# Loading p in one transfer and half of a k tile in fp32 by another queue, at the start of a packed-attention and token-mixing kernel

## The chip, the cores and the metric

The kernel runs on one core of one Trainium2 chip. The metric is the time of one launch in device microseconds, the median of several runs. A profile is one execution taken by the hardware profiler; its times count from the first instruction of that execution. The engines are TensorE (PE: matrix products; PEld: its weight loads), VectorE (DVE), ScalarE (ACT), GpSimd (POOL) and SyncE (SP). SyncE, ScalarE and GpSimd each issue transfers to a queue of their own; all queues are served by the core's 16 DMA engines.

## The reference

Two stages follow each other for 8 batches, 8 heads, 576 rows, head size 64 and 32 packing queries per head:

```python
p_packed = sm_attn(p, k, v)             # softmax(p k^T / 8) v : 32 rows per head
out      = sm_attn(q, p_packed, p_packed)
x = out.transpose(0, 2, 1, 3).reshape(8, 576, 512)
wq = x @ w_q; wk = x @ w_k              # 512 -> 64
W_tok = einsum('bsd,btd->bst', wq, wk) / 8
mixed = einsum('bst,btd->bsd', W_tok, x)
return maximum(mixed, 0) @ w_out        # float32, (8, 576, 512)
```

Inputs are float32; the kernel computes in bf16 with float32 accumulation.

## The kernel before

Everything is laid out by hand. `ORDER` is one long list of steps; each step is a name, indices, the engine that does it (`@V` VectorE, `@A` ScalarE, `@P` GpSimd, `@S` SyncE) and, after `=`, the PSUM banks. The loop at the end of the function issues the steps in that order, and each engine runs its own in that order; semaphores do the rest. Nothing is scheduled by a planner. Work of neighbouring batches is interleaved in the list, up to three batches deep.

The steps of one batch b, in their own order: `LD.k`, `LD.v`, `LD.q` load (GpSimd's queue casts fp32 to bf16 on the way); `KT` transposes k in blocks of 32 on VectorE; `S1` (line 282) makes the scores of p against k on TensorE; `X1` (line 293) takes the exponential on ScalarE; `TE` transposes it on VectorE; `PV` (line 315) multiplies with v; `RC` and `PP` normalise; `PT` transposes the packed result; `QK` multiplies it with the two small weights; `QV` transposes q; `S2`, `X2`, `RS`, `RR`, `AM`, `AT`, `AE` do the second attention; `WKQ`, `GM`, `Y`, `MX`, `RL`, `OT` (line 540), `OE`, `ST` the token mixing and the store. Stores on SyncE's queue are held until the last v has been loaded (`HOLD.v7`).

The part that the change touches is the start, before the scores of batch 0:

- p, 512 KB in fp32, is loaded once for all batches into a tile `p32` of 128 partitions x 1,024 elements (line 161) in two transfers: `LD.N0` on ScalarE's queue and `LD.N1` on SyncE's, 128 rows of 2 KB each. The source's extents are 16 (4 heads x 4 quarters of the 32 queries), 8 (batches) and 512 elements.
- `NC.0` on VectorE and `NC.1` on ScalarE cast a half each to bf16 (helper, lines 128 and 132); `PX.0` and `PX.1` (line 237) transpose the halves into `pT`, which the scores of all batches use.
- The two small weights follow on the same two queues: `LD.W0` on ScalarE's, `LD.W1` on SyncE's (line 164). GpSimd casts them in `WC.1` and `WC.0`, and stands still until they are there.
- k of batch 0 comes in two halves, both by GpSimd's queue: `LD.h0` (line 168) and `LD.g0` (line 157), then v, the two halves of q, and k of batch 1. `KT.0.0` and `KT.0.1` transpose the halves. `S1.0` needs both halves after its first two products.
- After its weight casts GpSimd issues k of batch 2, v of batch 1 and q of batch 1 (`LD.q1`, line 182), with fillings of constants between.
- `WARM.4=0` and `WARM.22.128=0` (line 619) are products of a constant tile with itself, one of 512 columns and 22 of 128, ahead of `S1.0`; further such fillings stand between the steps of batch 0, the next of them `WARM.8=4` between `S1.0` and `PV.0`.

Of the kernel before, what the change touches and what calls it, by code (L numbers as in the profile page):

```python
# [7 lines left out]
NL, NB, NO, NE = 4, 3, 6, 2  # L8
# [2 lines left out]
OHC = (0, 384), (384, 512)  # L11

ORDER = """
LD.N0@A LD.N1@S SET.warm@V SET.v0@V SET.aT0@V SET.aT1@V SET.aT2@V SET.idf@V LD.W0@A LD.W1@S SET.tab@A LD.h0
LD.g0 LD.v0 LD.r0 LD.q0 LD.k1 NC.0@V PX.0@V NC.1@A PX.1@V SET.aff@P SET.idb@V SET.v3@P KT.0.0@V SET.mask@P
WC.1@P WC.0@P LD.k2 SET.v1@P LD.v1 SET.v2@P KT.0.1@V WARM.4=0 WARM.22.128=0 S1.0=0,1,2,3 X1.0.1@A TE.0.1@V
X1.0.0@A TE.0.0@V WARM.8=4 PV.0.0=4,5 PV.0.1 RC.0@V PP.0.0@V PP.0.1@V LD.q1 PT.0@V WARM.6=6 QK.0=6 QKE.0@A
QV.0.0@V QV.0.1@V QD.0@P WARM.4=7 S2.0.2=2,3 X2.0.2@A RS.0.2@V RR.0.2@V S2.0.0=0,1 LD.v2 S2.0.1=4,5 X2.0.0@A
RS.0.0@V RR.0.0@V X2.0.1@A RS.0.1@V RR.0.1@V AM.0.2@P WARM.6=7 AT.0.2=7 AE.0.2@A AM.0.0@P WARM.5=6 AT.0.0=6
KT.1.2@V AM.0.1@P WARM.3=2 AT.0.1=7 AE.0.1@A AE.0.0@V WKQ.0.0=2,3 WKQ.0.2 WE.0.0@A LD.q2 WKQ.0.1 KT.2.2@V  # L20
S1.1=0,1,4,5 WE.0.1@A GM.0=6 X1.1.0@A TE.1.0@V GE.0@A WARM.2=7 Y.0=2,3 YE.0@V S1.2=0,1,6,7 MR.0=2,3 X1.1.1@A
TE.1.1@V MX.0.0=4,5 X1.2.0@A LD.O PV.1.0=0,1 TE.2.0@V PV.1.1 X1.2.1@A TE.2.1@V RC.1@V LD.k3 PP.1.0@V PP.1.1@V
PT.1@V MX.0.1=6,7 QV.1.2@V RLR.0@A QK.1=2 QKE.1@V RL.0.0@A WARM.3=3 S2.1.2=4,5 S2.1.0=0,1 RL.0.1@A X2.1.2@A
RS.1.2@V RR.1.2@V S2.1.1=2,3 X2.1.0@A RS.1.0@V RR.1.0@V WARM.1=6 PV.2.0=6,7 PV.2.1 X2.1.1@A RS.1.1@V RC.2@V
LD.v3 QD.1@P AM.1.2@P AT.1.2=4 RR.1.1@V AM.1.0@P WARM.5=5 AT.1.0=5 AM.1.1@P LD.k4 PP.2.0@V AE.1.2@A PP.2.1@V
PT.2@V QK.2=4 AE.1.0@A QKE.2@A QD.2@P QV.2.2@V LD.q3 LD.v4 AT.1.1=0 AE.1.1@A WKQ.1.0=2,3 WKQ.1.2 WKQ.1.1
WE.1.0@V S2.2.2=6,7 WE.1.1@A X2.2.2@A S2.2.3=4,5 X2.2.3@A GM.1=1 OT.0.0=2,3 GE.1@V Y.1=6,7 OT.0.1 YE.1@A
RS.2.4@V OE.0.0@A MR.1=0,1 MX.1.1=4,5 RLR.1@A RR.2.4@V OT.0.2=6,7 LD.q4 OT.0.3 KT.3.2@V AM.2.3@P OE.0.1@V
RL.1.1@A S1.3=2,3,0,1 X1.3.0@A AM.2.2@P OT.1.4=4 TE.3.0@V LD.k5 AT.2.2=5 X1.3.1@A TE.3.1@V AT.2.3=2 AE.2.3@V
LD.v5 MX.1.0=6,7 AE.2.2@V PV.3.0=0,1 PV.3.1 OEF.1.4@A WKQ.2.0=2,3 WKQ.2.1 RC.3@V PP.3.1@V RL.1.0@A WKQ.2.2  # L30
WE.2.2@A OT.1.2=4,5 OT.1.3 PP.3.0@V PT.3@V QK.3=6 OE.1.1@A LD.q5 KT.4.2@V S1.4=0,1,2,3 GM.2=7 OT.1.0=4,5
X1.4.1@A LD.k6 GE.2@A QKE.3@V X1.4.0@A QV.3.2@V TE.4.1@V Y.2=2,3 YE.2@A S2.3.2=6,7 X2.3.2@A S2.3.3=0,1
X2.3.3@A MX.2.0=2,3 TE.4.0@V RL.2.0@A MR.2=6,7 RLR.2@V OT.1.1 MX.2.1=6,7 RL.2.1@A OE.1.0@A PV.4.0=0,1 QD.3@P
PV.4.1 RS.3.4@V RR.3.4@V LD.v6 AM.3.3@P AM.3.2@P RC.4@V OT.2.0=2,3 OT.2.1 LD.q6 OE.2.0@A PP.4.0@V PP.4.1@V
PT.4@V QK.4=6 AT.3.3=7 QV.4.2@V AT.3.2=0 AE.3.2@A LD.k7 S2.4.2=4,5 AE.3.3@V X2.4.2@A S2.4.3=2,3 X2.4.3@A
# [25 lines left out]
def kernel(  # L61
# [27 lines left out]
    P = 128  # L89
# [64 lines left out]
    def load(x, eng):  # L154
        a, b = x[0], x[1:]
        if a == "g":
            nc.gpsimd.dma_start(k_in[0][:, 1], pairs(k, 0)[:, 1])
        elif a == "N":
            i, n = int(b), L * Dh // 4
            src = p.rearrange("b (i c) (z l) d -> i (c z) b (l d)", i=2, z=4)  # L160
            (nc.sync if eng == "S" else nc.scalar).dma_start(p32[:, i * n:(i + 1) * n], src[i])
        elif a == "W":
            w = (moe_w_k, moe_w_q)[int(b)].rearrange("(i c j e) m -> (c j) i (e m)", i=2, c=4, e=2)
            (nc.sync if eng == "S" else nc.scalar).dma_start(w32[:, int(b)], w)
        elif a == "O":
            nc.gpsimd.dma_start(wout, moe_w_out.rearrange("(j a) n -> a j n", a=P))
        elif a == "h":
            nc.gpsimd.dma_start(k_in[0][:, 0], pairs(k, 0)[:, 0])
        elif a == "v":
            b = int(b)  # L170
            for i in range(2):
                src = v[b, 4 * i:4 * i + 4].rearrange("c (g r) d -> g c (r d)", r=R)
                nc.gpsimd.dma_start(v_bufs[b % NL][halves(i), 0:7:2], src)  # L173
        elif a == "k":
            b = int(b)
            nc.gpsimd.dma_start(k_in[b % NL], pairs(k, b))
        elif a == "r" or x in ("q0", "q7"):
            b, i = int(b), int(a == "q")
            nc.gpsimd.dma_start(q_in[b % NL][:, i], pairs(q, b)[:, i])
        else:  # L180
            b = int(b)
            nc.gpsimd.dma_start(q_in[b % NL], pairs(q, b))
# [385 lines left out]

    def hold(x):
        b = int(x[1])  # L570
        src = {"k": k_in, "h": k_in, "q": q_in, "r": q_in, "v": v_bufs}[x[0]][b % NL]
        src = src[64:96, 4, 0:2] if x[0] == "v" else src[64:96, 0 if x[0] == "r" else 1, 0:2]
        z = 2 * int(x[0] == "h")
        nc.sync.dma_start(touch[:, z:z + 2], src)
# [78 lines left out]
```

## Time and profile before

| | |
|---|---|
| median of 3 runs | 104.46 us (104.32 to 104.92) |
| span of the profiled execution | 102.8 us |
| busy: TensorE, VectorE, ScalarE, GpSimd | 92.7, 73.7, 65.0, 51.8 us |
| bytes moved by the DMA engines | 25.13 MB, mean 244 GB/s |
| first product of the scores of batch 0 that uses k's second half | 10.18 us |
| batch 1's q landed | 27.48 us |

The profiled execution's own time is not listed apart from its span: the span runs from the first to the last instruction, and the timed runs are longer by what lies around it (104.46 against 102.8 us). In the rows of the profile a start and a length are given in us; `[idle before <-releaser]` is how long the engine stood still before the instruction, and what ended that. GB/s counts what the DMA engines write; a load that casts reads twice as much.

### The profile page before, as it was taken

What the parts mean: (1) busy time and instruction counts of PE and PEld (TensorE: products, weight loads), DVE (VectorE), ACT (ScalarE), POOL (GpSimd) and SP (SyncE); (2) the same over time, 40 slices, a digit from 0 to 9 for tenths busy, and PEclk for the clock granted to TensorE, in tenths of its full rate; (3) what the DMA queues carried; (4) which work ended last, traced back from release to release, by engine and by line L of the source; (5) the groups of instructions that cost most, each with busy time, mean ns of one, the idle gap of its engine ahead of it and who ended that gap; (6) DMA issues with size and microseconds to landing.
All of it is one profiled execution on the core that took longest, in us unless ns stands there. A gap on an engine that the chain in (4) does not pass through costs nothing.

```text
span 102.8 us, 3593 instructions
## 1 busy us (share of the span) xinstructions
PE 92.7 (90%) x1536; PEld 54.6 (53%) x1536; DVE 73.7 (72%) x140; ACT 65.0 (63%) x111; POOL 51.8 (50%) x81
## 2 busy tenths in 40 slices
PE   5995999998698899999998899989999999999940
PEld 3894454555364733655546556643757664743420
DVE  4173366966979479898597979689999979339520
ACT  2320406168853767938986979897889897735540
POOL 5971866993029938925349574558615009100000
PEclk9999999999999999999999999999999999999999
DMA  0999999999999999999999999999999999986894
GB/s 9 249 230 207 213 210 213 207 209 213 205 211 207 212 211 210 213 205 212 211 212 207 211 213 204 217 211 203 255 262 409 411 410 408 418 345 264 335 364 160
DMA packets 13279, 25.13 MB, mean 244 GB/s; under 512 B 1040, under 2 KB 6416, under 8 KB 13008
## 3 DMA queue, kind: packets, MB, share of 16 engines
q0 software_dynamic: 9648, 17.04, 84.0%
q1 hardware_dynamic: 3056, 7.41, 19.0%
q10 hardware_dynamic: 560, 0.46, 1.7%
q8 instruction: 12, 0.20, 0.7%
q14 instruction: 3, 0.02, 0.1%
HBM read 30.15 MB, written 9.44 MB: 385 GB/s over the span
## 4 chain that ended last, share of the span: by engine, by line
PE 49%; DMA 21%; DVE 8%; POOL 7%; ACT 6%; issue 3%; SPq 1%; DVEq 0%; POOLq 0%; ACTq 0%
PE ps L540 26%; DMA q_sb<-in_q_dram 13%; DMA o<-in_moe_w_q_dram 8%; PE ps L373 4%; POOL a L405 4%; PE ps L315 3%; ACT e1T L293 3%; PE ps L419 3%; PE ps L446 3%; DVE rs L394 2%; PE ps L441 2%; PE ps L467 2%; PE ps L282 2%; ACT e L378 1%; DVE qT L237 1%
## 5 line engine op out<-in xcount | busy, mean ns | idle before, releaser
L540 PE MATMUL ps<-wout,relu 128*128 128x512 bf16 x124 | 30.6, 380 | 0.0
L405 POOL TENSOR_TENSOR a<-e,rr 128x256 bf16<-128x256 f32 (+2 forms) x18 | 19.5, 1099 | 17.9 <-DVE rr L399 7.0
L619 PE MATMUL ps<-o 128*128 128x128 f32 (+3 forms) x76 | 19.5, 401 | 1.2 <-DVE o L135 1.2
L540 PEld LDWEIGHTS <-relu 128*128 128x128 bf16 x124 | 10.7, 98 | 11.7 <-issue 1.1
L128 ACT ACTIVATE o<-ps 128x1024 f32<-128x1024 f32 (+2 forms) x13 | 11.3, 871 | 5.4 <-PE ps L540 5.2
L619 PEld LDWEIGHTS ps<-o 128*128 128x128 f32 x76 | 11.3, 209 | 5.2 <-issue 3.6
L503 ACT ACTIVATE relu<-ps 128x1024 bf16<-128x1024 f32 (+1 forms) x14 | 13.0, 968 | 1.1 <-PE ps L492 1.1
L293 ACT ACTIVATE e1T<-ps 128x576 bf16<-128x576 f32 x16 | 9.8, 656 | 5.8 <-PE ps L282 5.2
L378 ACT ACTIVATE e<-ps 128x256 f32<-128x256 f32 (+2 forms) x19 | 11.2, 623 | 2.7 <-PE ps L373 2.5
L394 DVE TENSOR_REDUCE rs<-e 128x16 f32<-128x512 f32 (+2 forms) x13 | 10.9, 840 | 2.3 <-ACT e L378 2.2
L237 DVE STREAM_TRANSPOSE kT<-k_sb 128x1152 uint32<-128x1152 uint32 (+1 forms) x9 | 11.1, 1230 | 1.9 <-DMA k_sb<-in_k_dram 1.9
L173 POOL DMA_DIRECT2D v_sb<-in_v_dram x16 | 10.0, 628 | 4.0 <-DMA v_sb<-in_v_dram 1.6
L237 DVE STREAM_TRANSPOSE qT<-q_sb 128x1152 uint32<-128x1152 uint32 (+1 forms) x10 | 11.0, 1108 | 0.1
L132 DVE COPY o<-ps 128x1024 f32<-128x1024 f32 (+2 forms) x7 | 6.8, 977 | 5.3 <-PE ps L540 2.7
L237 DVE STREAM_TRANSPOSE e<-e1T 128x288 uint32<-128x288 uint32 x16 | 7.4, 468 | 3.1 <-ACT e1T L293 2.7
L128 ACT ACTIVATE aT<-ps 128x128 bf16<-128x128 f32 (+2 forms) x11 | 5.0, 465 | 5.7 <-PE ps L419 3.3
L128 ACT ACTIVATE wkq<-ps 128x448 bf16<-128x448 f32 (+1 forms) x10 | 7.2, 730 | 1.8 <-PE ps L446 1.7
L315 PE MATMUL ps<-v_sb,e 64*64 64x192 bf16 x288 | 7.5, 245 | 0.8 <-DVE e L237 0.5
L315 PEld LDWEIGHTS <-e 64*64 64x64 bf16 x288 | 5.9, 107 | 2.6 <-DVE e L237 2.1
L373 PEld LDWEIGHTS <-qT 64*128 64x128 bf16 x320 | 5.4, 94 | 2.8 <-DVE qT L237 1.7
L373 PE MATMUL ps<-ppT,qT 64*128 64x64 bf16 x320 | 6.6, 190 | 0.2 <-DVE qT L237 0.2
L446 PE MATMUL ps<-aT,pqk 128*128 128x256 bf16 (+1 forms) x48 | 6.8, 246 | 0.0
(70 smaller groups left out, 130.3 us busy)
## 6 DMA issues: line engine op xcount, KB each, us to landing
v_sb<-in_v_dram POOLq DMA_DIRECT2D x16, 288.0 KB, 13.9
out_dram<-o SPq DMA_DIRECT2D x9, 512.0 KB, 9.3
k_sb<-in_k_dram POOLq DMA_DIRECT2D x7, 576.0 KB, 13.6
q_sb<-in_q_dram POOLq DMA_DIRECT2D x6, 576.0 KB, 13.6
out_dram<-o POOLq DMA_DIRECT2D x2, 1024.0 KB, 11.3
out_dram<-o SPq DMA_DIRECT2D x5, 256.0 KB, 2.5
q_sb<-in_q_dram POOLq DMA_DIRECT2D x4, 288.0 KB, 10.4
out_dram<-orem SPq DMA_DIRECT2D x3, 256.0 KB, 8.5
```

The lines of the kernel that those rows point to most:

```text
L128: nc.scalar.activation(o, i, COPY)
L173: nc.gpsimd.dma_start(v_bufs[b % NL][halves(i), 0:7:2], src)
L237: nc.vector.transpose(o, i)
L293: nc.scalar.activation(e1T[:, x], T["s1", b][x].rearrange("a c m -> a m c"), EXP, scale=scale)
L315: nc.tensor.matmul(T["pv", b][halves(cc), i], lhsT, rhs, start=n == 0, stop=n == R - 1, skip_group_check=True)
L373: nc.tensor.matmul(ps[:, y, t - t0, i], lhsT, rhs, start=e == 0, stop=e == 1)
L378: nc.scalar.activation(e2[:, t0:t1].rearrange("a t (i y n) -> a y (t i) n", i=2, y=2), T["s2", b, c].rearrange("a y t i n -> a y (t i) n") ...
L394: nc.vector.tensor_reduce(rs[:, t0 * H:t1 * H], src, axis=AX, op=ADD)
L405: e.tensor_tensor(a2[:, t0:t1].rearrange("a t i (u l) -> a (t i u) l", l=L), e2v(b, c), T["rr", b][:, t0 * H:t1 * H].to_broadcast((P, (t1 ...
L503: nc.scalar.activation(o, i, RELU)
L540: nc.tensor.matmul(ps, lhsT, wout[:, j, :], start=j == 0, stop=j == NJ - 1)
L619: nc.tensor.matmul(bank(int(bk), [w]), warm[:, 0:P], rhs, start=True, stop=True)
```

## The change

p is loaded by one transfer on ScalarE's queue, `LD.N`, with rows of 4 KB. The source's extents are then 8 (4 heads x 2 halves of the 32 queries), 16 (batches x 2 groups of heads) and 1,024 elements. The transposes `PX` read and write in the matching order; `PX.0` and `PX.1` both still handle half of the elements each, and `NC.0`, `NC.1` stay as they were.

The first half of batch 0's k is loaded in fp32 by SyncE's queue (`LD.H0`, 128 rows of 4,608 B) into `h32`, a part of an output tile that is free until batch 4, and cast to bf16 by ScalarE (`HC`, 128 x 1,152), after its cast of p. GpSimd's queue has one issue less and begins with k's second half. SyncE's weight transfer now stands behind half of k instead of half of p, ScalarE's behind all of p.

22 filling products of 128 columns ahead of the scores become 17. The rest of `ORDER` is the same.

```diff
-LD.N0@A LD.N1@S SET.warm@V ... LD.W0@A LD.W1@S SET.tab@A LD.h0
-LD.g0 LD.v0 LD.r0 LD.q0 LD.k1 NC.0@V PX.0@V NC.1@A PX.1@V SET.aff@P SET.idb@V ...
-... WARM.4=0 WARM.22.128=0 S1.0=0,1,2,3 ...
+LD.N@A LD.H0@S SET.warm@V ... LD.W0@A LD.W1@S SET.tab@A LD.g0 LD.v0
+LD.r0 LD.q0 LD.k1 NC.0@V NC.1@A PX.0@V PX.1@V HC@A SET.aff@P SET.idb@V ...
+... WARM.4=0 WARM.17.128=0 S1.0=0,1,2,3 ...
...
-            i, n = int(b), L * Dh // 4
-            src = p.rearrange("b (i c) (z l) d -> i (c z) b (l d)", i=2, z=4)
-            (nc.sync if eng == "S" else nc.scalar).dma_start(p32[:, i * n:(i + 1) * n], src[i])
+            src = p.rearrange("b (i c) (z l) d -> (c z) (b i) (l d)", i=2, z=2)
+            (nc.sync if eng == "S" else nc.scalar).dma_start(p32, src)
+        elif a == "H":
+            (nc.sync if eng == "S" else nc.scalar).dma_start(h32, pairs(k, 0)[:, 0])
...
-        elif a == "h":
-            nc.gpsimd.dma_start(k_in[0][:, 0], pairs(k, 0)[:, 0])
...
+    h32 = spare[:, 0:RQ * Dh]
...
-               .rearrange("a (b i z l) -> a i l z b", b=B, i=2, z=4)[:, x],
-               pbf.bitcast(u32).rearrange("a (i l z b) -> a i l z b", i=2, b=B, z=4)[:, x])
+               .rearrange("a (u z x l) -> a x l z u", u=2 * B, z=2, x=2)[:, x],
+               pbf.bitcast(u32).rearrange("a (x l z u) -> a x l z u", x=2, z=2, u=2 * B)[:, x])
+
+    def HC(eng, bk):
+        copy(eng, k_in[0][:, 0], h32)
```

More of the change, by code (lines that the diff above doesn't have):

```diff
@@ L13 @@
 ORDER = """
[L14 to L23, printed above, removed]
@@ L54 @@
-STF.6.3 YE.7@A ST.5.0 MR.7=6,7 RLR.7@A MX.7.0=4,5 RLF.7.0.1@A RLF.7.0.0@V MX.7.1=2,3 RLF.7.1.0@A OT.7.4=0
-OEF.7.4@A ST.7.4 RLF.7.1.1@V OT.7.1=6 OEF.7.1@V OT.7.0=7 STF.7.1 OT.7.2=1 OEF.7.0@A OH.7.0=0 STF.7.0 OEF.7.2@A
-STF.7.2 OEH.7.0@V STH.7.0 OH.7.1=5 OEH.7.1@A STH.7.1@A
+LD.N@A LD.H0@S SET.warm@V SET.v0@V SET.aT0@V SET.aT1@V SET.aT2@V SET.idf@V LD.W0@A LD.W1@S SET.tab@A LD.g0 LD.v0
+LD.r0 LD.q0 LD.k1 NC.0@V NC.1@A PX.0@V PX.1@V HC@A SET.aff@P SET.idb@V SET.v3@P KT.0.0@V SET.mask@P WC.1@P WC.0@P
@@ L57 @@
+WKQ.7.1 WE.7.0@A WE.7.1@A STF.6.2 OT.6.0=6,7 OT.6.1 GM.7=0 OE.6.0@V OT.5.1 OE.5.0@V ST.5.1 GE.7@A Y.7=4,5 OT.6.3
+OEF.6.3@V ST.6.0 STF.6.3 YE.7@A ST.5.0 MR.7=6,7 RLR.7@A MX.7.0=4,5 RLF.7.0.1@A RLF.7.0.0@V MX.7.1=2,3 RLF.7.1.0@A
+OT.7.4=0 OEF.7.4@A ST.7.4 RLF.7.1.1@V OT.7.1=6 OEF.7.1@V OT.7.0=7 STF.7.1 OT.7.2=1 OEF.7.0@A OH.7.0=0 STF.7.0
+OEF.7.2@A STF.7.2 OEH.7.0@V STH.7.0 OH.7.1=5 OEH.7.1@A STH.7.1@A
 """
@@ L570, in hold @@
         b = int(x[1])
[L571 removed]
+        src = {"k": k_in, "q": q_in, "r": q_in, "v": v_bufs}[x[0]][b % NL]
         src = src[64:96, 4, 0:2] if x[0] == "v" else src[64:96, 0 if x[0] == "r" else 1, 0:2]
[L573 to L574 removed]
+        nc.sync.dma_start(touch[:, 0:2], src)
     def OH(b, h, eng, bk):
```

65 lines of the change are left out of this document (35 added, 30 removed).

## The prediction

> **What bounds the kernel now.** I read the page first, then the chain that ended last, then the start of the timeline, then the DMA by stretches of a microsecond.
>
> ```profile
> span 102.8 us, 3593 instructions
> PE 92.7 (90%) x1536; PEld 54.6 (53%) x1536; DVE 73.7 (72%) x140; ACT 65.0 (63%) x111; POOL 51.8 (50%) x81
> GB/s 9 249 230 207 213 210 213 207 209 213 205 211 207 212 211 210 213 205 212 211 212 207 211 213 204 217 211 203 255 262 409 411 410 408 418 345 264 335 364 160
> q10 hardware_dynamic: 560, 0.46, 1.7%
> 13.89 13.59 DMA q_sb<-in_q_dram
> 27.48 0.02 issue
> 27.51 1.39 DVE qT L237
> ...
> 98.09 0.67 PE ps L580 x4
> ```
>
> The first four lines are the page's; the rest is the chain (start, length, what). TensorE (PE) is busy 90% of the span, and after 28.9 us nearly every piece of the chain is compute: no load ends a step there. Before it there is one long piece, the load of batch 1's q, which lands at 27.48. The loads run at about 210 GB/s from the second slice on. That counts what is written, and a casting load writes half of what it reads. Stores reach 410 GB/s. So both cases move about 410 GB/s, and a load that sits in a full queue comes when the bytes ahead of it are through, not when it was issued.
>
> Is that load the only thing that ends there? The timeline of VectorE (DVE) just before, and the chain's start on all engines:
>
> ```profile
> 27.14 0.31 DVE L237 STREAM_TRANSPOSE ppT<-pp 128x128 uint32<-128x128 uint32 x1
> 0.73 0.65 ACTq L161 DMA_DIRECT2D o<-in_p_dram  x1
> 0.74 0.68 SPq L161 DMA_DIRECT2D o<-in_p_dram  x1
> 1.27 0.73 POOL L168 DMA_DIRECT2D k_sb<-in_k_dram  x1 [0.82 <-POOLq L637]
> 3.06 5.60 PEld L619 LDWEIGHTS ps<-o 128*128 128x128 f32 x43 [0.52 <-issue]
> 4.66 0.48 DVE L132 CAST o<-o 128x512 bf16<-128x512 f32 x1 [2.53 <-DMA o<-in_p_dram]
> 5.18 0.65 DVE L237 STREAM_TRANSPOSE pT<-o 128x256 uint32<-128x256 uint32 x1
> 5.76 0.63 ACT L128 ACTIVATE o<-o 128x512 bf16<-128x512 f32 x1 [2.21 <-DMA o<-in_p_dram]
> 6.42 0.64 DVE L237 STREAM_TRANSPOSE pT<-o 128x256 uint32<-128x256 uint32 x1 [0.60 <-ACT o L128]
> 6.92 0.21 DVE L204 CAST idb<-o 128x128 bf16<-128x128 f32 x1
> 7.04 0.78 DVE L237 STREAM_TRANSPOSE kT<-k_sb 128x576 uint32<-128x576 uint32 x1
> 8.78 0.29 PE L282 MATMUL ps<-kT,pT 32*32 32x288 bf16 x2
> 9.34 0.78 DVE L237 STREAM_TRANSPOSE kT<-k_sb 128x576 uint32<-128x576 uint32 x1 [1.52 <-DMA k_sb<-in_k_dram]
> 9.84 0.74 POOL L130 CAST wqk<-o 128x256 bf16<-128x256 f32 x2 [2.46 <-DMA o<-in_moe_w_q_dram]
> 10.18 0.47 PE L282 MATMUL ps<-kT,pT 32*32 32x288 bf16 x30 [1.10 <-DVE kT L237]
> 10.58 1.98 PE L619 MATMUL ps<-o 128*128 128x512 f32 x4
> 12.51 0.94 PE L315 MATMUL ps<-v_sb,e 64*64 64x192 bf16 x36
> ```
>
> The transpose of batch 1's packed result ends at 27.14 + 0.31 = 27.45, and the transpose of q starts at 27.51: the compute side and the load arrive within 0.03 us of each other. So the change pays only if it brings forward both, and it costs as soon as either is late. The compute side hangs on the scores of batch 0 (10.18): from there exponentials, VectorE transposes, the product with v (12.51) and the rest follow each other without a load ending a step. What opens 10.18 is the second transpose of k (9.34 + 0.78), which waited 1.52 us for k's second half. The filling products were done before 8.78 and hide nothing there.
>
> **The change, part by part.** The terms come from these rows. The first four stand in the stretches 2 to 3, 3 to 4 (two rows) and 4 to 5 us (packets, MB); the fifth is the stretch 12 to 14; then the DMA issues (KB, us to landing) and ScalarE's (ACT) groups by shape (busy, mean ns).
>
> ```profile
> q10 hardware_dynamic: 40, 0.08, 51.5%
> q1 hardware_dynamic: 62, 0.13, 47.9%
> q10 hardware_dynamic: 104, 0.18, 47.3%
> q0 software_dynamic: 41, 0.09, 49.0%
> DMA packets 204, 0.41 MB, mean 207 GB/s; under 512 B 24, under 2 KB 24, under 8 KB 204
> o<-in_p_dram ACTq DMA_DIRECT2D x1, 256.0 KB, 3.9
> o<-in_p_dram SPq DMA_DIRECT2D x1, 256.0 KB, 5.0
> L503 ACT ACTIVATE relu<-ps 128x1024 bf16<-128x1024 f32 x12 | 11.9, 1029 | 1.1 <-PE ps L492 1.1
> L503 ACT ACTIVATE relu<-ps 128x512 bf16<-128x512 f32 x2 | 1.1, 598 | 0.0
> ```
>
> q10 is ScalarE's queue, q1 SyncE's (SP), q0 GpSimd's (POOL). ScalarE's moves from 2 us on, SyncE's only after 3, GpSimd's only after 4.
>
> *Row times.* 410 GB/s over 16 engines is 25.6 GB/s each: a 4 KB row takes 160 ns, an fp32 k row of 4,608 B 180 ns. GpSimd's casting rows: 204 - 24 = 180 in 2 us on 16 engines, 178 ns. So moving half of k to SyncE costs the DMA nothing by itself.
>
> *p in one transfer.* The doubtful point is how many engines carry it. Before, the source's extents were 16, 8 and 512 elements; now they are 8, 16 and 1,024, because 4 KB rows leave only (4 heads) x (2 halves) outermost. On q10 there were three transfers (half of p, one weight, the last store): 128 + 256 + 128 = 512 rows, and 560 - 512 = 48 packets remain, 16 end marks each, one per engine. All their outer extents divide by 16. None of before has an outer extent of 8, so the trace bounds it from both sides: 16 engines with 8 rows each, or 8 engines with 16 rows each. I take 8, since a cut along the outermost extent has no more pieces to hand out, and keep 16 for the range.
> The Trainium skill, "DMA: Bandwidth & Descriptors", section "Why a DMA increments its semaphore by 16 and not by 1", says that a transfer uses the largest count up to 16 that divides the slowest extent on both sides, which is 8 here; no run here shows it yet.
>
> With 8 engines: by 3.0 us 40 rows are on their way, 5 per engine, 11 left. From 3 to 4 SyncE's k rows alternate with them (160 + 180 = 340 ns): 3 rounds, 8 left. From 4 GpSimd's rows take a turn too (518 ns): five rounds to 6.6, when k's 8 rows are through; the last 3 go with GpSimd's and the weights' at some 360 ns, to 7.7. Landing follows the last row by 0.7 us: q10's 40 + 104 = 144 packets (128 rows, 16 marks) were all out by 4.0, and p landed at 0.73 + 3.9 = 4.63. So p lands at 8.4 instead of 4.63 and 0.74 + 5.0 = 5.74. That rows take strict turns is my assumption; if p went first throughout, it would land at 3.0 + 11 x 0.16 + 0.7 = 5.5, but then k's 8 rows would run from 4.8 beside GpSimd's (358 ns) and land at 8.4.
>
> *The cast of k on ScalarE.* From 598 to 1,029 ns for 512 more elements: 0.84 ns each; 1,152 elements with the 631 ns base of 512 in the timeline (0.63) make 0.63 + 640 x 0.84 = 1.17 us. It stands behind the cast of p's second half (0.63). ScalarE's next work is the exponential after the scores, so nothing else waits behind it.
>
> *From landing to scores.* With p at 8.4: ScalarE's two casts end at 8.4 + 0.03 + 0.63 + 1.17 = 10.2. VectorE meanwhile does its cast (0.52 from start to start), two transposes of p (0.50 each) and the identity (0.12), done at 10.1; it is hidden by a hair. Then two transposes of k, 0.78 each, to 11.8, and scores at 11.9: 1.7 us after 10.18. If p goes first: k lands at 8.4, cast to 9.6, transposes to 11.2, scores 1.0 later. If the weights slow the end more, p at 9.0 gives 2.3 later.
>
> *q of batch 1.* Each of the eight engines now moves 16 x 160 = 2.56 us of p instead of 16 x 80 = 1.28. Against it, 2.2 to 4.0 was half empty (40 + 166 packets of 2 KB are 0.4 of the 0.74 MB that fit), which gives back 0.8. It lands some 0.5 us later, at 28.0, and is covered by compute, which now comes at 27.45 + 1.7 = 29.15.
>
> *GpSimd* drops one issue of 0.73 us, so its loads up to batch 1's k are issued earlier. Its weight casts (9.84) wait for SyncE's weight, now behind half of k; behind them are queued k of batch 2, v and q of batch 1. q of batch 1 was issued 13.6 us before it landed, in a full queue, so a delay of 1 to 2 us there costs nothing; without that backlog it would cost itself.
>
> *Five filling products fewer.* 43 loads in 5.60 us, two per product, are 0.26 us each: 1.3 us less TensorE work, ending at about 7.5 instead of 8.8. Nothing waits for it, so it gains nothing.
>
> **Sum.** Scores, and all of the compute chain behind them, come 1.7 us later; after 28.9 the chain has no slack that could take it up. The profiled execution has a span of 102.8 us; the median of the three runs is 104.46, 1.66 beyond the span, which I carry over: 104.5 + 1.66 = 106.2 us.
>
> **Rivals.** (1) *The p transfer uses all 16 engines, and the kernel gets faster.* 40 rows by 3.0 are 2.5 per engine; 5.5 left; 3 rounds to 4.0, 2.5 rounds of 518 to 5.3: p lands at 6.0. k's half ends at 6.2 to 6.3, lands at 7.0, is cast by 8.2, transposed with the other half by 9.8: scores at 9.9, 0.3 earlier. Without GpSimd's turns (its rows were slow to start, 41 from 4 to 5) k's half would end at 4.0 + 2.5 x 0.34 + 2.5 x 0.18 = 5.3 and scores come at 8.8; then batch 1's q is the later one, which the regained empty time brings forward by up to 0.8. Faster by 0.3 to 0.8: I take 103.8. For it: the half empty stretch is real. Against it: the outer extent. It decides if p lands before 6 and k before 6.8.
> (2) *16 engines, but no gain*: k's half lands at 7.3 because turns are strict and the weights come between; scores at 10.2, time 104.4.
> (3) *8 engines and a slow TensorE clock.* The filling now ends at 7.5 and scores come at 11.9: 4.4 us idle.
>
> ```profile
> 98.90:102.80 3.90, 0.07 (x2) 0.00 (x0) 0.51 (x1) 0.28 (x1) 0.00 (x0) 1.00 0.64 232
> 2.20 0.34 PEld L619 LDWEIGHTS ps<-o 128*128 128x128 f32 x1 [0.52 <-issue]
> 13.91 0.19 PEld L619 LDWEIGHTS ps<-o 128*128 128x128 f32 x1 [0.24 <-issue]
> ```
>
> In the last 3.9 us TensorE did next to nothing and the granted clock stayed at 1.00, which speaks against; but 4.4 is longer, and the same weight load took 0.34 us at the start against 0.19 later, so a slow state exists. There the 0.47 of scores and the 1.98 of filling behind them would take 0.34/0.19 = 1.8 times as long, 1.9 us more, ahead of the product with v: 108.1. It decides from the idle length at which the clock falls.
> The Trainium skill, "TensorE: Matmul & The Clock Gate", section "Part 1: The HAM clock gate", gives a free-running window of about 3.4 us without work for that fall; by it 4.4 us idle may or may not hold a whole window, and this trace's 3.9 us at 1.00 agree with the second.
>
> **How the numbers follow.** Forecast (8 engines, clock kept) 0.60; slow clock 0.13; 16 engines without gain 0.14; 16 engines and faster 0.13. About 0.5%, 0.5 us, is what a measurement of this kernel tells from no change, so slower 0.73, same 0.14, faster 0.13. The forecast's own range is 105.4 to 106.8 (scores 1.0 to 2.3 later). To hold 8 in 10 it has to take in the case without gain and much of the slow clock: 104.1 to 107.8.
>
> **What the changed profile would show.** Right: ScalarE's queue with 8 fewer end marks than a full transfer, p landing 7 to 8 us after its issue, the cast of k at 9 to 10 us, scores near 11.9, batch 1's q transposed near 29.2 with VectorE, not the load, ending that wait. Wrong: p landing before 6 us, scores before 10.2, or the later chain taking up the delay.

## The result, and the profile after

The changed kernel takes 113.31 us (median of 4 runs, 112.81 to 114.06), the kernel before on the same chip 104.44 us: 1.084 times as long, interval 1.0789 to 1.0891. The forecast was 106.2 us, its range ended at 107.8. The sign was right, the size was not.

The page of the changed kernel, whose profiled execution took 114.06 us, the longest of the four: span, busy times, the granted clock in 40 slices, ScalarE's queue.

```profile
span 112.3 us, 3555 instructions
PE 93.7 (83%) x1511; PEld 54.7 (49%) x1526; DVE 73.2 (65%) x140; ACT 66.1 (59%) x112; POOL 51.3 (46%) x80
PEclk9999555699999999999999999999999999999996
q10 hardware_dynamic: 552, 0.72, 3.3%
```

TensorE's busy time is 1.0 us more than before (92.7), the span 9.5 us more: TensorE waited. PEclk shows where: four slices of 2.8 us each, from 11 us on, at five to six tenths of the clock. q10 has 552 packets where before had 560: 8 end marks instead of 16 for p's transfer, so 8 engines.

The longest piece of the chain of waits (first line) and the timeline of the start (start, length, engine, line; `[idle before <-releaser]`):

```profile
0.73 11.85 DMA o<-in_p_dram
0.73 1.26 ACTq L158 DMA_DIRECT2D o<-in_p_dram  x1
0.74 0.39 SPq L160 DMA_DIRECT2D o<-in_k_dram  x1
1.19 6.64 PE L619 MATMUL ps<-o 128*128 128x512 f32 x36 [1.19 <-DVE o L133]
12.61 0.63 ACT L126 ACTIVATE o<-o 128x512 bf16<-128x512 f32 x1 [8.64 <-DMA o<-in_p_dram]
12.61 0.43 DVE L130 CAST o<-o 128x512 bf16<-128x512 f32 x1 [10.49 <-DMA o<-in_p_dram]
13.15 1.15 ACT L126 ACTIVATE k_sb<-o 128x1152 bf16<-128x1152 f32 x1
14.33 1.44 DVE L235 STREAM_TRANSPOSE kT<-k_sb 128x576 uint32<-128x576 uint32 x2
15.16 0.42 PE L283 MATMUL ps<-kT,pT 32*32 32x288 bf16 x2 [7.33 <-DVE kT L235]
15.82 0.70 PE L283 MATMUL ps<-kT,pT 32*32 32x288 bf16 x30 [0.24 <-DVE kT L235]
16.45 3.78 PE L619 MATMUL ps<-o 128*128 128x512 f32 x4
20.17 1.65 PE L316 MATMUL ps<-v_sb,e 64*64 64x192 bf16 x36
35.78 1.33 DVE L235 STREAM_TRANSPOSE qT<-q_sb 128x1152 uint32<-128x1152 uint32 x1
```

p was issued at 0.73 and landed at 12.58. (Below, p's landing is the start of its casts, 0.03 us later.) Everything of the start hangs on it: the casts at 12.61, the cast of k's half behind one of them, the two transposes of k, the scores at 15.82 instead of 10.18. TensorE had nothing from 7.83 to 15.16. Then the same work took longer: scores 0.70 us (0.47 before), four filling products 3.78 (1.98), the product with v 1.65 (0.94), 2.74 us together. Batch 1's q, which ended a wait before, no longer does: its transpose at 35.78 follows VectorE's own work.

The DMA queues in the stretches 2 to 3 (first line), 3 to 4 (two), 4 to 5 (two), 9 to 10 (two) and 10 to 11 us (last line): packets, MB, share of the 16 engines' time.

```profile
q1 hardware_dynamic: 67, 0.31, 82.9%
q1 hardware_dynamic: 137, 0.25, 69.7%
q10 hardware_dynamic: 21, 0.09, 21.8%
q10 hardware_dynamic: 27, 0.11, 52.9%
q0 software_dynamic: 8, 0.02, 19.4%
q0 software_dynamic: 82, 0.11, 86.7%
q10 hardware_dynamic: 17, 0.05, 30.2%
q10 hardware_dynamic: 28, 0.03, 18.1%
```

Now SyncE's queue (q1, half of k) moves first; p's rows (q10) begin only after 3. From 4 to 5 they take 52.9% of 16 engines, half of them full, for 27 rows: 0.529 x 16 / 27 = 0.31 us a row. From 3 to 4 it was 0.218 x 16 / 21 = 0.17 us. From 9 to 10 there are 17 packets, but 0.05 MB: at most 13 of them can be rows of p, the others are short, so 8 / 13 = 0.6 us or more passed from row to row on each engine, beside GpSimd's casting rows (q0). The mean packet falls to 1 KB in 10 to 11: p's last 4 KB rows end there, 1.6 us or more before the landing.

The granted clock over the start of the changed kernel (stretch, length, busy time of PE, PEld, DVE, ACT, POOL, then PEclk, DMA share, GB/s):

```profile
10.00:12.00 2.00, 0.00 (x0) 0.00 (x0) 0.00 (x0) 0.00 (x0) 0.00 (x0) 0.90 1.26 171
12.00:14.00 2.00, 0.00 (x0) 0.00 (x0) 1.35 (x4) 1.39 (x2) 0.40 (x1) 0.50 1.17 212
20.00:22.00 2.00, 2.00 (x38) 1.56 (x38) 0.10 (x1) 0.00 (x0) 0.00 (x0) 0.54 1.12 200
```

A mean of 0.90 from 10 to 12 is 0.4 us at half clock, so it fell at 11.6, and 0.54 from 20 to 22 puts its return at 21.84: 10.24 us at half clock.

Up to the reciprocal after the first product with v the kernel is 8.37 us late (13.53, now 21.90): 5.64 by the scores' start, 2.74 by the clock. It stays so to the last store's issue (99.44, now 108.04: 8.60). The rest is at the very end (experiments 8 to 11).

### The profile page after: what moved, and what is told of

The parts are those of the page before. It is cut to its first block, busy times and chain, and to the rows that moved or that the text cites. A ratio compares the mean times of both kernels' runs of the same rounds, so it can differ in the third digit from the quotient of the medians.

```text
span 112.3 us, 3555 instructions
## 1 busy us (share of the span) xinstructions
PE 93.7 (83%) x1511; PEld 54.7 (49%) x1526; DVE 73.2 (65%) x140; ACT 66.1 (59%) x112; POOL 51.3 (46%) x80
## 4 chain that ended last, share of the span: by engine, by line
PE 62%; DMA 11%; DVE 9%; ACT 8%; issue 4%; POOL 3%; DVEq 0%; POOLq 0%; ACTq 0%
PE ps L541 23%; DMA o<-in_p_dram 11%; PE ps L619 10%; PE ps L316 5%; PE ps L374 4%; PE ps L283 3%; POOL a L406 3%; PE ps L420 3%; ACT e1T L294 3%; PE ps L447 3%; DVE kT L235 2%; PE ps L468 2%; DVE rs L395 2%; PE ps L442 2%; PE ps L337 2%
## 5 line engine op out<-in xcount | busy, mean ns | idle before, releaser
L541 PE MATMUL ps<-wout,relu 128*128 128x512 bf16 x112 | 29.5, 380 | 0.9 <-issue 0.3
L619 PE MATMUL ps<-o 128*128 128x128 f32 (+3 forms) x66 | 20.3, 452 | 1.2 <-DVE o L133 1.2
L619 PEld LDWEIGHTS ps<-o 128*128 128x128 f32 x66 | 10.8, 222 | 6.2 <-issue 4.7
L395 DVE TENSOR_REDUCE rs<-e 128x16 f32<-128x512 f32 (+2 forms) x13 | 10.9, 841 | 2.3 <-ACT e L379 2.2
L283 PE MATMUL ps<-kT,pT 32*32 32x288 bf16 x256 | 4.5, 308 | 7.9 <-DVE kT L235 7.9
L235 DVE STREAM_TRANSPOSE kT<-k_sb 128x1152 uint32<-128x1152 uint32 (+1 forms) x9 | 10.9, 1224 | 0.2
L235 DVE STREAM_TRANSPOSE qT<-q_sb 128x1152 uint32<-128x1152 uint32 (+1 forms) x10 | 10.9, 1102 | 0.0
L316 PE MATMUL ps<-v_sb,e 64*64 64x192 bf16 x288 | 8.4, 260 | 1.0 <-DVE e L235 0.5
L128 POOL COPY pqk<-pqk 128x128 bf16<-128x128 bf16 x8 | 2.3, 289 | 14.1 <-DVE pqk L130 9.2
L316 PEld LDWEIGHTS <-e 64*64 64x64 bf16 x288 | 6.5, 114 | 3.7 <-issue 2.4
L130 DVE CAST o<-o 128x512 bf16<-128x512 f32 x1 | 0.4, 427 | 10.5 <-DMA o<-in_p_dram 10.5
```

The costliest lines, as they stand in the source:

```text
L235: nc.vector.transpose(o, i)
L283: nc.tensor.matmul(T["s1", b][c % 2][quarter(2 * i + gh), c // 2], pT[quarter(c), 2 * b + i, :, e], kT[quarter(c), i, :, gh * 32:(gh + 1) ...
L316: nc.tensor.matmul(T["pv", b][halves(cc), i], lhsT, rhs, start=n == 0, stop=n == R - 1, skip_group_check=True)
L395: nc.vector.tensor_reduce(rs[:, t0 * H:t1 * H], src, axis=AX, op=ADD)
L541: nc.tensor.matmul(ps, lhsT, wout[:, j, :], start=j == 0, stop=j == NJ - 1)
L619: nc.tensor.matmul(bank(int(bk), [w]), warm[:, 0:P], rhs, start=True, stop=True)
```

## The experiments

Fourteen kernels, each given with the kernel that its edit starts from. Theories at the start: A, p on 8 engines is late and TensorE's clock falls meanwhile; B, half of k by SyncE's queue and its cast hold the start up; C, five fewer filling products let the clock fall.

### 1. p on 16 engines (from the changed kernel)

```diff
-src = p.rearrange("b (i c) (z l) d -> (c z) (b i) (l d)", i=2, z=2)   # 8 x 16 rows of 4 KB
+src = p.rearrange("b (i c) (z l) d -> (c z) b i (l d)", i=2, z=4)     # 16 x 8 x 2 rows of 2 KB
```

The transposes `PX` follow the layout of before.

> The changed kernel, with p still in one transfer on ScalarE's queue but as 256 rows of 2 KB whose source has an outermost extent of 16. Theory A (the outermost extent of 8 puts p on 8 of the 16 DMA engines, so p lands late and TensorE cools while it waits): 16 end marks on ScalarE's queue instead of 8, p lands at 5.5 to 6.5 us instead of 12.6, scores by 10.5, no slice with a lowered clock, 103.7 to 104.8 us. Theory B (half of k in fp32 on SyncE's queue and its cast by ScalarE hold the start up): p still lands after 9 us and the time stays above 109. Theory C (the five fillings fewer let the clock fall by themselves): the clock still falls for some microseconds after 8, time 106 to 107.

Measured: 105.29 us, 1.0066 times before (1.0041 to 1.0091). Page, ScalarE's queue from 3 to 4 us, and timeline:

```profile
q10 hardware_dynamic: 688, 0.72, 2.7%
q10 hardware_dynamic: 77, 0.16, 42.1%
6.80 0.43 DVE L130 CAST o<-o 128x512 bf16<-128x512 f32 x1 [4.68 <-DMA o<-in_p_dram]
10.01 0.47 PE L283 MATMUL ps<-kT,pT 32*32 32x288 bf16 x30 [0.36 <-DVE kT L235]
```

688 packets are 128 more rows and 8 more end marks than 552. p landed 5.8 us earlier, with half of k, its cast and the 17 fillings unchanged, and 8.0 of the 8.9 us are gone. That is A. The edit also halves p's rows, but from 3 to 4 us a row of 2 KB took 0.421 x 16 / 77 = 0.09 us here and one of 4 KB 0.17 us in the changed kernel, the same per byte; rows of 4 KB on 16 engines were not run. Scores now come 0.17 us earlier than before, and the time is still 0.7% longer: something else costs. (One of the four executions took 107.07 us at a mean granted clock of 0.975; experiment 9 shows such a one.)

### 2. p on 8 engines alone (from the kernel before)

```diff
-LD.N0@A LD.N1@S
+LD.N@A                      (8 x 16 rows of 4 KB, PX to match; k by GpSimd, 22 fillings)
```

> The kernel before, with nothing changed but p: one transfer of 4 KB rows with an outermost extent of 8 on ScalarE's queue, no half of k on SyncE's, all 22 fillings. Theory A: 8 end marks, p lands at 9 to 12 us, scores at 12.5 to 15.5; idle after the filling 4 to 7 us, so the clock falls too; 108 to 113 us. Theory B: p lands near 6, 104 to 105 us. Theory C: with all the fillings the clock holds, and only the late scores cost: 107 to 109.

Measured: 109.53 us, 1.0469 (1.0406 to 1.0532). p landed at 8.6, near the forecast's 8.4 and earlier than the 9 to 12 expected by A; then k's second half came late as well, scores at 12.78 on a fallen clock:

```profile
12.78 0.71 PE L281 MATMUL ps<-kT,pT 32*32 32x288 bf16 x30 [1.61 <-DVE kT L236]
```

So p on 8 engines costs 5.2 us by itself, and 4 us more of p's lateness come with the rest of the change.

### 3. Half of k alone (from the kernel before)

```diff
-LD.N0@A LD.N1@S ... LD.h0
+LD.N0@A LD.H0@S LD.N1@A ... HC@A     (both halves of p on ScalarE's queue, 16 engines each)
```

> The kernel before, with p in its two transfers of 16 outermost pieces, both on ScalarE's queue, half of batch 0's k in fp32 on SyncE's queue with the cast on ScalarE, all 22 fillings. Theory A: p lands by 6.5, k's half by 5, scores at 8.9 to 10, batch 1's q lands 0.3 to 0.8 earlier than 27.5, 103.6 to 104.4 us. Theory B: 107 us or more, scores after 12. Theory C: as A.

Measured: 108.13 us, 1.0375 (1.0318 to 1.0432), which seemed to speak for B. But p's second half was cast only at 8.71: its transfer stood second on ScalarE's queue, and there it came 3 us later than on SyncE's. Scores at 11.92, and the fillings behind them took 3.18 us. The experiment changed p's queue with k's, so it doesn't try B alone. Experiment 8 does: half of k on SyncE's queue with p in one transfer on 16 engines costs nothing.

### 4. Filling up to the scores (from the changed kernel)

```diff
-WARM.17.128=0
+WARM.52.128=0
```

> The changed kernel with 52 instead of 17 filling products of 128 columns ahead of the scores, which at 0.22 us each end at about 15.4 us, when p and k are ready. Theory A with the clock as a second price: p lands at 12.6 as in the changed kernel, no lowered clock, the filling between scores and the product with v takes 2.0 instead of 3.8 us, and the time is 2.5 to 3 us below the changed kernel's, 110.3 to 110.9. If the lowered clock cost nothing on the path: the same 113.3. Theory C (the clock is the main cause): 105 to 106.

Measured: 109.69 us, 1.0517 (1.0479 to 1.0556). p landed at 11.09; TensorE was filled until 15.3, 1 us past the point where k's transposes were ready; the clock stayed at 1.00, the scores took 0.48, the fillings behind them 1.98, the product with v 0.94:

```profile
15.27 0.48 PE L283 MATMUL ps<-kT,pT 32*32 32x288 bf16 x32
```

Though scores came only 0.55 us earlier, 3.6 us are gone: the idle clock was a price of its own, on top of the wait. (0.9 us of the 3.6 belong to experiments 8 to 11.)

### 5 and 6. Less beside p on the hardware queues (from the changed kernel)

```diff
-LD.N@A LD.H0@S ... LD.W0@A LD.W1@S
+LD.N@A LD.H0@S ... LD.W0@A LD.W1@A      (5: moe_w_q behind moe_w_k)
+LD.N@A LD.H0@A ... LD.W0@A LD.W1@A      (6: all on ScalarE's queue, p first)
```

> The changed kernel with one move: the load of moe_w_q is issued by ScalarE behind moe_w_k, no longer by SyncE behind half of k. So nothing but half of k stands on SyncE's queue while p loads. Two theories of why p lands at 12.6 us in the changed kernel and at 8.6 us where only its own transfer was changed. Start theory: the two hardware queues hand out their transfers one after the other in order of issue, and p's first row (3.5 us) waits for what SyncE issued before ScalarE's longer issue was through; then p's first row comes at 2.5 to 3.0 us and p lands near 11. Sharing theory: p's eight engines give turns to each other queue's rows, whatever the start; then the first row stays near 3.5 us, and p lands 1 to 2 us earlier because 16 weight rows an engine go behind p instead of between. Both give 110.5 to 112.5 us; the first row tells them apart. If neither holds, p lands at 12.6 us and the time stays at 113.

> The changed kernel with p, half of k, moe_w_k and moe_w_q all issued by ScalarE, in this order; SyncE loads nothing. p has its eight engines to itself until GpSimd's rows come at 4 to 5 us. Sharing and start theory together: first row of p near 2.6 us, p lands at 6.5 to 8 us, as far as GpSimd's rows allow; half of k follows it in the queue and lands at 8.5 to 9.5 us, is cast to 10.5, scores at 12 to 12.5 us, 106.5 to 108.5 us, with or without a slow clock. If p's eight engines are slow by themselves (a row takes 0.4 us or more even alone), p lands at 9 or later, half of k at 11, and the time is 110 or more.

Measured: 111.28 us, 1.0621 (1.0585 to 1.0658), and 112.58 us, 1.0746 (1.0708 to 1.0783). In 5, p's first rows were no earlier (13 packets from 3 to 4 us, 21 in the changed kernel), so the weight ahead was not what they waited for; p landed at 10.87, 1.7 us earlier, as the sharing theory had it. How much of that is the edit is less sure: with all loads as in the changed kernel p landed at 11.09 in experiment 4 and at 11.82 in 10. In 6:

```profile
9.59 0.43 DVE L130 CAST o<-o 128x512 bf16<-128x512 f32 x1 [7.47 <-DMA o<-in_p_dram]
13.05 1.16 ACT L126 ACTIVATE k_sb<-o 128x1152 bf16<-128x1152 f32 x1 [2.83 <-DMA o<-in_k_dram]
15.73 0.70 PE L283 MATMUL ps<-kT,pT 32*32 32x288 bf16 x30 [0.24 <-DVE kT L235]
```

p went first and landed 3.0 us earlier, and half of k came 8.3 us later: the scores are where they were (15.73 against 15.82).

### 7. Half of k cast ahead of p (from experiment 1)

```diff
-NC.0@V NC.1@A PX.0@V PX.1@V HC@A ... KT.0.0@V
+HC@A KT.0.0@V NC.0@V NC.1@A PX.0@V PX.1@V ...
```

> The kernel with p as 256 rows of 2 KB in one transfer (16 engines) and half of k on SyncE's queue, with the order of the casts changed: ScalarE casts half of k (landed at 4.7 us) before its half of p, and VectorE transposes that half of k ahead of p. In the run before, p landed at 6.8, and the casts of p and k stood one behind the other on ScalarE (0.63 + 1.15 us) before the first transpose of k at 8.5. Expected: cast of k 4.8 to 5.9, transpose to 6.7, p cast at 6.8, second transpose of k (its load lands at 7.9) at 8.3 to 9.1, scores at 9.1 us, 0.9 earlier than 10.0. If the compute chain sets the end: 104.0 to 104.6 us. If batch 1's q (landing near 27) then is the later one, or a later stall takes it back, 104.5 to 105.3 us. Theory B (the cast of half of k holds the start up) expects the full 0.9 us.

Measured: 104.92 us, 1.0035 (1.0014 to 1.0056). Scores at 9.31, 0.70 earlier than in experiment 1, of which 0.37 us are left in the time. So the cast on ScalarE did stand on the path (B), for 0.7 us; yet with scores 0.87 us earlier than before the kernel is no faster than before.

### 8. p on 16 engines with 22 fillings (from experiment 1)

```diff
-WARM.17.128=0
+WARM.22.128=0
```

> The kernel with p as 256 rows of 2 KB in one transfer (16 engines) and half of k on SyncE's queue, with the 22 filling products of the kernel before instead of 17. Filling then ends at 10.1 us instead of 8.8, beside scores that were ready at 10.0. Theory C (fewer filling products let the clock fall in some executions; one of four ran at a mean granted clock of 0.975 and 107.07 us): all runs at 0.99 or above, none over 105.5. If filling plays no part: 105.2, spread as before, or 0.1 to 0.2 more since filling may end after the scores are ready.

Measured: 104.06 us (103.94 to 104.10), 0.9952 (0.9935 to 0.9969): 0.5% faster than before, and 1.2 us faster than with 17. The start is the same as with 17 (scores at 9.98 and 10.01), and so is every step up to 68 us. The first of the differences is on TensorE at that point of experiment 1, in the middle of one product with v, where the kernel with 22 doesn't stop:

```profile
67.97 0.77 PE L316 MATMUL ps<-v_sb,e 64*64 64x192 bf16 x28 [0.47 <-DVE e L235]
69.18 0.36 PE L316 MATMUL ps<-v_sb,e 64*64 64x192 bf16 x8 [0.44 <-issue]
```

The second is at the end. Experiment 1: the queue that loads code (q8) in the stretch 95 to 96 us, SyncE's store issues, and the last stores (KB, us from issue to landing):

```profile
q8 instruction: 1, 0.02, 5.9%
96.19 1.17 SPq L560 DMA_DIRECT2D out_dram<-orem  x1
99.46 0.54 SPq L590 DMA_DIRECT2D out_dram<-o  x1
out_dram<-o SPq DMA_DIRECT2D x1, 192.0 KB, 3.3
out_dram<-o ACTq DMA_DIRECT2D x1, 64.0 KB, 3.0
```

The same with 22 fillings, where the code packet is in the stretch 91 to 92:

```profile
q8 instruction: 1, 0.02, 6.4%
95.52 0.34 SPq L560 DMA_DIRECT2D out_dram<-orem  x1
98.80 0.54 SPq L590 DMA_DIRECT2D out_dram<-o  x1
out_dram<-o SPq DMA_DIRECT2D x1, 192.0 KB, 2.5
out_dram<-o ACTq DMA_DIRECT2D x1, 64.0 KB, 2.0
```

One packet of code takes 0.059 x 16 = 0.94 us of an engine. With 17 fillings the last one comes some 3.5 us before the last store's issue, with the stores already moving. SyncE's issue of `orem`, which falls beside it, takes 1.17 us instead of 0.34, and the last stores land 0.8 to 1.0 us later.

### 9. 17 fillings alone (from the kernel before), 10. 22 in the changed kernel, 11. 17 wide ones (from experiment 1)

```diff
-WARM.22.128=0            -WARM.17.128=0            -WARM.17.128=0
+WARM.17.128=0   (9)      +WARM.22.128=0   (10)     +WARM.26.196=0   (11: 17 products of 196 columns)
```

> The kernel before with one change: 17 filling products instead of 22 ahead of the scores. Two theories of why, with p on 16 engines and half of k on SyncE's queue, 17 products gave 105.2 us and 22 gave 104.06. Code theory: five products are 20 instructions of TensorE; with them gone, TensorE's last 16 KB of code is fetched 3 to 4 us before the last store instead of 6 to 8 us, amid the closing stores, which then land 0.8 to 0.9 us later; at about 68 us a code fetch may also stop TensorE for 0.4 us. Then 105.2 to 105.7 us here too, with a closing store that lands 3.3 us after issue instead of 2.5. Clock theory: filling keeps TensorE's clock up only where the scores come after it; then the time differs from 104.4 only in runs of a lower granted clock, and the closing stores land after 2.5 us.

> The changed kernel with 22 filling products instead of 17: only the third part of the change is undone. Code theory: 0.8 to 1.3 us less than 113.3, so 112.0 to 112.5, the closing store lands 2.5 us after its issue; start and scores as in the changed kernel (p lands between 11 and 12.6 us, slow clock from 12 to 20). Clock theory: filling then ends 1.2 us later, at 9.1, but p still comes 2 to 3 us after that, so the clock falls all the same and the time stays at 112.8 to 114.

> p as 256 rows of 2 KB in one transfer, half of k on SyncE's queue, and 17 filling products of 196 columns in place of 17 of 128: as many instructions as with 17, and filling that lasts about as long as with 22 of 128 (to 9 us or later). Code theory: what counts is the number of instructions, so 105.0 to 105.4 us as with 17 of 128, the closing store landing after 3.3 us. Clock theory: what counts is how long TensorE is filled, so 104.0 to 104.2 us as with 22.

Measured: 9: 105.72 us, 1.0131 (1.0092 to 1.017). 10: 111.12 us, 1.0655 (1.0623 to 1.0686). 11: 105.33 us, 1.0093 (1.007 to 1.0116).

Experiment 11 decides between the length of the filling and the number of its instructions: as many instructions as 17 narrow products, TensorE filled without a gap to the scores, clock 1.00 throughout its profile, and it is as slow as 17 (105.33 against 105.29), with a stop of 0.51 us in the same product with v and closing stores that land after 3.2 and 2.9 us. So the number counts. The table holds for every kernel here, from its profiled execution:

| kernels | fillings | code packet to last store's issue | last 192 KB land after |
|---|---|---|---|
| changed, experiments 1, 5, 6, 7, 9, 11 | 17 | 3.5 to 3.6 us | 3.2 to 3.4 us |
| before, experiments 2, 3, 4, 8, 10, 12, 13, 14 | 22 (4: 52) | 6.0 to 11 us | 2.4 to 2.5 us |

That the packet's place makes the stores late is what I infer from the two going together; which engine's code it holds no row says, though only TensorE's instruction count was changed.

Theory C has a share too. Two of the six executions of 9 ran at a mean clock of 0.975 or 0.974 and took 106.66 and 107.26 us, while the one at 1.000 took 105.24. The profiled one is of the first kind:

```profile
9.80 0.47 PE L282 MATMUL ps<-kT,pT 32*32 32x288 bf16 x30 [1.65 <-DVE kT L237]
10.00:11.00 1.00, 1.00 (x32) 0.49 (x3) 0.00 (x0) 0.63 (x2) 1.00 (x3) 0.95 1.22 210
14.00:15.00 1.00, 1.00 (x25) 0.77 (x18) 0.17 (x1) 0.00 (x0) 0.54 (x1) 0.85 1.14 219
```

The longest gap was 1.65 us, and the clock was at half from 10.9 to 14.3 us. In 10, 2.2 us came back, more than the 1.3 that the code theory allowed. The closing stores gave 0.9 us of the profiled difference (3.4 us from the last store's issue to the end, 4.3 in the changed kernel). The start gave the rest: p landed 0.8 us earlier (11.82), though its loads are the same, and the clock was at half for 6.8 us instead of 10.2. Whether that is the filling's doing or differs from execution to execution no run here shows.

### 12. Cast first, 22 fillings (from experiment 7)

```diff
-WARM.17.128=0
+WARM.22.128=0
```

> p as 256 rows of 2 KB in one transfer, half of k on SyncE's queue and cast by ScalarE ahead of p, and 22 filling products. With 17 products and this order scores came at 9.3 us, 0.7 ahead of the other order, but behind batch 1's q (which landed at 27) only 0.1 us of it was left. So 103.9 to 104.1 us by the code theory, 1 us under the same order with 17 products (104.9), and as good as equal to 104.06; a version that beats both kernels only if the load of batch 1's q comes earlier as well.

Measured: 103.64 us (103.53 to 104.07), 0.9933 (0.9911 to 0.9954): the best version here, 0.7% faster than before, and 1.3 us faster than the same order with 17 fillings. The gain stops where the expectation put it, at batch 1's q:

```profile
26.82 1.38 DVE L235 STREAM_TRANSPOSE qT<-q_sb 128x1152 uint32<-128x1152 uint32 x1 [0.21 <-DMA q_sb<-in_q_dram]
```

### 13 and 14. What makes p land 4 us later than alone (from experiment 10)

```diff
-LD.N@A LD.H0@S ... LD.W1@S
+LD.N@A LD.W1@S LD.H0@S ...                                          (13)
-LD.g0 LD.v0 ... SET.aff@P ... SET.v3@P ... SET.mask@P ... SET.v1@P ... SET.v2@P
+SET.v3@P SET.mask@P SET.v1@P SET.v2@P SET.aff@P LD.g0 LD.v0 ...     (14)
```

> The changed kernel with 22 filling products, and on SyncE's queue the load of moe_w_q ahead of half of k instead of behind it. The same transfers on the same queues in another order. Start theory (the second hardware queue's rows begin only when the first one's first transfer has been handed out): SyncE's first transfer is now 256 rows of 512 B, handed out from 1.75 to 2.6 us, where half of k took until 3.7; p's first row then comes at 2.5 us instead of 3.5, some 50 p rows are out by 4.0 instead of 21, p lands at 8.6 to 9.8, half of k (now beside p) at 7 to 9, scores at 11.5 to 13, and the time is 107.5 to 109.5, against 111.12 with half of k first. Sharing theory (the start does not matter, the rows beside p on its eight engines do): half of k's rows now run beside p, so p lands at 11 or later, and the time is 110.5 or more.

> The changed kernel with 22 filling products, in which GpSimd does its five settings (memsets and the mask) ahead of its loads, so that its first load is issued some 3 us later (4.3 us instead of 1.27) and its rows come at 7 us instead of 4. Only p's landing is asked for; the other loads are late. Sharing theory: from 3.5 to 7 us p's eight engines carry little beside p, a 4 KB row takes 0.2 us as where p was alone (37 rows in the stretch 3 to 4 us, 0.22 us a row and engine), and p lands at 7.5 to 8.5. If the lateness has to do with the start only: p's first row at 3.5 us as before, and p lands at 10.5 or later.

Measured: 13: 111.97 us, 1.0738 (1.0677 to 1.0799); 14: 110.06 us, 1.0534 (1.05 to 1.0568). In 13, SyncE's short weight rows are through by 3 us, and p's rows begin there (stretch 2 to 3):

```profile
q1 hardware_dynamic: 236, 0.14, 71.0%
q10 hardware_dynamic: 8, 0.03, 49.3%
12.69 0.43 DVE L130 CAST o<-o 128x512 bf16<-128x512 f32 x1 [10.57 <-DMA o<-in_p_dram]
```

So the order of the first transfers sets p's start, but an earlier start gained nothing: p landed at 12.69, with half of k now beside it, which landed at 12.0 instead of 4.7. The start theory falls. In 14 GpSimd's first load was issued 2.3 us later than in 10 (3.57 against 1.26), but its rows began only 1.5 us later (5.9 against 4.4), not 3 as meant:

```profile
10.56 0.43 DVE L130 CAST o<-o 128x512 bf16<-128x512 f32 x1 [8.43 <-DMA o<-in_p_dram]
```

p landed 1.3 us earlier than in 10, where the sharing theory expected 3 to 4, and 0.5 earlier than in 4, whose loads are those of 10. The 10.5 or later that was expected if only the start mattered fits, but 13 speaks against that. So neither theory holds as it was put, and what GpSimd's rows cost p is not settled.

What remains: scores came at 15.82, 15.73, 15.03 and 15.90 in the changed kernel and experiments 6, 10 and 13, whichever of p and half of k went first. Taking other rows away brings p forward: half of k in experiment 2 (GpSimd loads it there), perhaps GpSimd's in 14 and the weight's in 5; changing the order of p and k does not bring the scores forward. That fits eight engines that have p's sixteen rows each besides their share of all else, but the rows of the queues don't name single engines, so it isn't shown engine by engine. Why p landed at 11.09, 11.82 and 12.61 with the same loads stays open.

## Why the prediction was right and wrong, step by step

*Eight engines*: right. The end marks say so (552 packets against 560, and 688 in experiment 1), and so does the 52.9% of 16 engines that p's rows took from 4 to 5 us. This agrees with the rule that the prediction took from the Trainium skill, "DMA: Bandwidth & Descriptors", section "Why a DMA increments its semaphore by 16 and not by 1".

*p lands at 8.4*: wrong by 4.2 us, the largest mis-sized term. Three parts of its working failed.

- *The rows out by 4.0 us.* The prediction had 8 of each engine's 16 rows out, 64 in all; 21 were. It let ScalarE's queue move from 2.2 us, as before, but p's issue now took 1.26 us instead of 0.65, SyncE's first one 0.39, and SyncE's transfer went first: p's first row came after 3.4. It also carried the 40 rows of 2 KB that 16 engines had out by 3.0 over as 40 rows of 4 KB on 8 engines, which is twice the bytes on half the engines; in experiment 6, where p went ahead of all other loads, 25 were out by then.
- *The pace after that.* The other 107 rows took until nearly 11 us: 7.0 x 8 / 107 = 0.52 us from row to row on each engine. The prediction's round of three queues was the same 0.518 us, but it had only five of them, and 0.36 us for each of the last three rows.
- *The landing.* It came 1.6 us or more after the last row, not 0.7.

On each engine 5.4 more rows were left at 4.0 us, 2.8 us at 0.52; the slower end of the other eight is 0.5, the landing 0.9: together the 4.2 us. An earlier start alone would not have given the 2.8 back: in experiment 13 p's rows began 1 us earlier, beside half of k, and p landed no earlier. The row itself, put at 160 ns from the stores at full rate, took 0.17 us from 3 to 4, as put, and 0.31 from 4 to 5. That is not peculiar to the eight engines: in experiment 1 the rows of 2 KB on 16 engines took 0.135 us each then, which is 0.27 for 4 KB (stretch 4 to 5):

```profile
q10 hardware_dynamic: 122, 0.25, 103.2%
```

What lengthens them, and so what makes up the 0.52 us, stays open. That p landed at 8.6 in experiment 2, without half of k beside it, is near 8.4 by luck: the working had half of k beside p.

*Landing to scores, 3.5 us*: right; 3.24 measured. The cast of k took 1.15 us (1.17 forecast).

*Clock kept*: wrong, and so the forecast was chosen over rival 3, to which I gave 0.13. The choice between them went by how long TensorE may idle, for which the end of before, 3.9 idle us at full clock, was the row against the rival. The idle length alone doesn't decide: in the changed kernel the clock fell 3.8 us after the last filling at the start (7.83 to 11.6), and 3.0 us after the last product at the end, where the kernel before idled 3.9 us without a fall:

```profile
107.00:108.00 1.00, 0.57 (x7) 0.31 (x4) 0.55 (x1) 0.60 (x2) 0.00 (x0) 1.00 0.93 348
110.00:111.00 1.00, 0.00 (x0) 0.00 (x0) 0.00 (x0) 0.00 (x0) 0.00 (x0) 0.79 0.15 51
```

The last product ends at 107.57, and a mean of 0.79 from 110 to 111 puts the fall at 110.58. The rival's price was nearly right as far as it went: 1.9 us for scores and filling, 2.03 measured; it left out the product with v (0.71 us).

*Five fillings fewer, "nothing waits for it, so it gains nothing"*: wrong, at a place the prediction never looked at. It costs 0.8 to 1.3 us (experiments 8, 9, 12), at 68 us in some kernels and at the closing stores in all; the code load as its cause is inferred.

*q of batch 1 covered, GpSimd's delay free*: right, but hardly tried; at 35.78 the transpose of q waited for no load, with the compute before it 8 us late.

*Rivals 1 and 2, 16 engines*: experiment 8, which differs from the kernel they priced by the 22 fillings, gave scores at 9.98 (rival 1: 9.9) and 104.06 us, between their 103.8 and 104.4. p landed later there than rival 1 had it (6.8 against 6.0).

The profiled execution ends at 114.06, 7.9 over the forecast: 3.9 by the later scores (4.2 - 0.3), 2.7 by the clock, 0.9 by the closing stores, 0.2 between the reciprocal and the last store, where TensorE stopped twice for 0.2 us near 78 us, and 0.2 unexplained.

## What to carry to other kernels

Before merging transfers into longer rows, look at the outermost extent that is left: with 8 the transfer here ran on half the engines and landed 3 us later by itself, 7 with half of k beside it. A load that starts a kernel has two prices, the wait and the clock that TensorE loses while it waits; fillings pay for the second only if they last until the data is there. And a handful of instructions more or fewer can move a code load by microseconds, so compare the closing stores too before a difference of 1% is put down to the edit's purpose.

## What the runs showed of the hardware

- The half-clock stretches were 3.4 us long in experiment 9, 6.8 in 10 and 10.2 in the changed kernel: one, two and three times the same length. This agrees with the window of about 3.4 us of the Trainium skill, "TensorE: Matmul & The Clock Gate", section "Part 1: The HAM clock gate".
- The same section speaks of an idle window before the fall, and the measurement differs: in experiment 9 TensorE was busy for 1.4 of the 3.4 us before it (estimated from the stretches of half a microsecond), with no gap over 1.65 us, and the clock fell in two of six executions.
- Of the first transfers of the two hardware queues, one had a good part of its rows out before the other's began, and it was the one whose issue ended first: half of k (issue 0.39 us) ahead of p (1.26 us) in the changed kernel, 81 of 128 rows by 3 us; p's one half ahead of its other in the kernel before, 40 of 128 by 3 us.
- Issuing p with an outermost extent of 8 took 1.22 to 1.26 us, with 16 it took 0.66 to 0.68, for the same 512 KB.
